# Windowed attention and routed experts on one core: first v queued ahead, gate exp moved behind the third score piece, key copies placed on ScalarE or VectorE by the chunk before, last gate ahead of the row check

## The chip, the core and the metric

The kernel runs on one core of a Trainium2 chip. The time is that of one execution on the device, in microseconds; shorter is better. Engine names are those of the profile: PE is TensorE's matmul, PEld its weight load, DVE is VectorE, ACT is ScalarE, POOL is GpSimd, SP is SyncE.

## The reference

There are 8 batches of 8 heads, 576 positions and head size 64. Attention is causal with a window of 64 positions; its output becomes a row of 512 per position. Then each batch as a whole goes to one of 8 experts, chosen by the mean of its rows. All inputs and the output are float32.

```python
rel = pos[:, None] - pos[None, :]
mask = (rel >= 0) & (rel < 64)
scores = np.where(mask, scale * q @ k.T, -1e9)
attn = exp(scores - max) / (sum + 1e-9)
x = (attn @ v) as (B, S, 512)
...
logits = x.mean(axis=1) @ w_gate
e = argmax(logits); gate_w = softmax(logits)[e]
out[b] = gate_w[b] * (relu(x[b] @ w1[e]) @ w2[e])     # w1 512x1024, w2 1024x512
```

## The kernel before

**Units.** The attention is cut into 16 units u, two for each batch (four heads each, as two pairs s). For a unit, `load_qk` brings q and k as bfloat16 over POOL's DMA queue. `transpose_qk` transposes them on PE into one PSUM tile each, and `leave_qk` copies that tile out: q always on ACT, k on DVE unless ACT is passed. `scores(u, c)` makes the scores of a third (piece) c of the window blocks, and ACT takes the exp of each piece into `pt` (L389). The window is applied in one of two ways: units 0 and 1 add a large negative number on PE before the scores (`add_outside`, into the same PSUM tile); the others multiply the exp by 0 or 1 on DVE (L391, with `masks` from `make_masks`). `values(u, s)` is the second product, of `pt` with v; its 65th column is the row sum, and `norm` divides on DVE (L427, L429) and writes x.

**v.** `load_v(b)` loads a batch's v as float32 over SP's queue. A small POOL instruction first writes one element of the tile, so that the DMA waits for POOL at that place. `cast_part` converts it to float16 twice, in two alignments: "whole" (`va`), and "low" and "high" (`vb`); `cast_v` does all three for a unit.

**Gate.** `transpose_x` transposes x for the expert, ACT summing each row on the way out (`pooled`), and `gate_parts` multiplies the sums with the gate's weights. For batch 0 `pool_mm` and `pool_parts` do this in another way, ahead of the transposes. `gate(b)` finishes the logits with a matmul into PSUM (L488), takes the maximum and its index on DVE (L492 to L495), and loads the index into a POOL register, with which `load_w1` and `load_w2` ask for that expert's weights. `gate_weight(b)` takes the exp and the sum of the logits on ACT (L515) and the reciprocal on DVE (L517). The expert's relu (L562) scales by it.

**Experts.** `expert_chunks` yields, batch after batch, 8 `expert_up` chunks (64 matmuls of 128x288 in all, relu on ACT) and 5 `expert_down` chunks (the output copied by DVE, L575 and L587, and stored over SP's queue). `experts(pace)` issues the next chunks of this stream, so that expert work fills PE between the pieces of attention.

**Order.** Every instruction is kept in program order on its engine (`P`), so the order of the text is the order of each engine's queue. A hand-written lead-in takes units 0 to 3 and the first gate; it holds `busy(n)`, matmuls on zeros that only occupy PE. Then a loop over t handles unit t's scores and values, the transposes of unit t+1, the transpose of x of unit t-1, and at even t (from 6 on) the gate of batch t/2 - 1. At t = 16 (`NU`) there is no unit left; the last gate is done, and `row_check` tests all row sums on DVE for a general fallback, which is not taken here. All PSUM tiles come from one pool of four:

```python
psum = ctx.enter_context(
    tc.tile_pool(name="psum", bufs=4, space=bass.MemoryType.PSUM))
```

so a fifth tile must wait until one of the four is read out.

Of the kernel before, what the change touches and what calls it, by code (L numbers as in the profile page):

```python
# [156 lines left out]
def kernel(  # L157
# [61 lines left out]
    def load_v(b, behind=None):  # L219
        vn = vpool.tile([128, NM, D], FP32, tag="vn")  # L220
        if behind is None:

            P(nc.gpsimd.memset(vn[:, 0, 0:1], 0.0))
        else:

            P(nc.gpsimd.tensor_copy(out=vn[:, 0, 0:1], in_=behind))
        P(nc.sync.dma_start(out=vn, in_=vv[b]))
        v_tiles[b] = vn

    HM = NM // 2  # L230

# [123 lines left out]
    sp_ps = {}  # L355

    def add_outside(u, c):

        sp = psum.tile([128, 2, 512], FP32, tag="ps", name="sp")
# [4 lines left out]
        sp_ps[u, c] = sp  # L364

    def scores(u, c):
        qT, kT = qt_tiles[u], kt_tiles[u]
        masked = (u, c) in sp_ps
        if not masked:
            sp_ps[u, c] = psum.tile([128, 2, 512], FP32, tag="ps", name="sp")  # L370
        sp = sp_ps[u, c]
# [114 lines left out]
    def gate(b, both=True):  # L486
        gl = psum.tile([128, 2, 512], FP32, tag="ps")
        P(nc.tensor.matmul(out=gl[:, 0, 0:E], lhsT=onesf, rhs=gparts[b],  # L488
                           start=True, stop=True))
        glog = gl[:, 0, 0:E]  # L490
# [9 lines left out]
        gate_in[b] = gl, gnm  # L500
        if both:
            gate_weight(b)
# [7 lines left out]
    def gate_weight(b):  # L510
        gl, gnm = gate_in[b]
        glog = gl[:, 0, 0:E]
# [53 lines left out]
    def expert_down(b, mt):  # L566
# [3 lines left out]
        if mt < 4:  # L570
# [4 lines left out]
            P(nc.vector.tensor_copy(out=ob, in_=pso[:, 0, :]))  # L575
# [50 lines left out]
    acc = [0.0]  # L626
# [49 lines left out]
    busy(13)  # L676
    transpose_qk(0, 0)
    add_outside(0, 0)
    transpose_qk(0, 1)
# [15 lines left out]
    cast_v(1)  # L695
# [4 lines left out]
    values(0, 0)  # L700
    values(0, 1)
    transpose_qk(2, 0)
    busy(1)
# [5 lines left out]
    busy(1)  # L709
    pool_mm(1)  # L710
    pool_parts()
    gate(0, False)
# [6 lines left out]
    for c in range(3):  # L719
        scores(2, c)  # L720
        if c == 0:
            gate_weight(0)
# [7 lines left out]
    busy(3)  # L730
# [12 lines left out]
    values(3, 1)  # L743
    experts(1.0)
    transpose_qk(4, 0)
    transpose_qk(4, 1)
    experts(1.0)
    transpose_x(3)

    for t in range(START + 1, NU + LAG):  # L750
# [22 lines left out]
        if t == NU:  # L773
            okc = row_check()
# [3 lines left out]
        if t == START + 1:  # L778
            next_gate()
        if ahead and t > 5:  # L780
            cast_part(t + 1, "low")
        if on:
            scores(t, 1)
        if ahead and t > 5:
            cast_part(t + 1, "high")
        experts(pace)
        if START + 1 < t <= NU and t % 2 == 0:
            next_gate()
        if on:
            scores(t, 2)  # L790
        if t == START + 1:
# [8 lines left out]
        if ahead:  # L800
            transpose_qk(t + 1, 1)
# [47 lines left out]
```

## Time and profile before

| | |
|---|---|
| Time, median of 3 runs | 235.32 us (233.7 to 235.49) |
| Time of the profiled execution | 234.69 us |
| Its span, first to last instruction | 233.0 us |
| Mean granted TensorE clock | 0.981 |
| PE busy | 205.6 us (88%) |
| PE weight load busy | 142.2 us (61%) |
| DVE busy | 140.1 us (60%) |
| ACT busy | 122.5 us (53%) |
| POOL busy | 41.2 us (18%) |
| DMA | 45.64 MB, mean 196 GB/s |

All times in the traces are counted from the start of the span. The time of the execution is 1.69 us longer than its span. A row of the timeline has start, duration, engine, line, operation, output<-inputs, and in brackets how long the engine stood idle before it and what ended that. A row of the groups ends with busy time and mean duration in ns, then the idle time before, and for whom.

### The profile page before, as it was taken

Reading aid. Unit: us, or ns where it says so; the run is one execution under the profiler, and the core shown is the slowest. Engines: PE = TensorE matmul, PEld = TensorE weight load, DVE = VectorE, ACT = ScalarE, POOL = GpSimd, SP = SyncE. Lnnn points to the kernel's source line nnn. Section 1 sums busy time; section 2 is a strip of 40 time slices with the busy share of each in tenths; the row PEclk is TensorE's granted clock in tenths of the full one; section 3 lists DMA queues with packets and bytes.
Section 4 is the critical chain, followed back from the end, with each engine's and each line's share of the span. In section 5 each row is a group of like instructions: output and inputs, shape, how many; then the busy total and the mean of one; then the engine's idle time right before and its main releaser. Section 6 shows DMA issues by size and latency. Waiting matters only on the chain.

```text
span 233.0 us, 6978 instructions
## 1 busy us (share of the span) xinstructions
PE 205.6 (88%) x3012; PEld 142.2 (61%) x3012; DVE 140.1 (60%) x314; ACT 122.5 (53%) x206; POOL 41.2 (18%) x69
## 2 busy tenths in 40 slices
PE   7656889999799899989999899999998999979970
PEld 2335767745587557855686457856686568639630
DVE  2639596578757777478656777467766672440140
ACT  2344686851668338670957356853677247406300
POOL 7146260055000330025000700020002000200000
PEclk9999599999999999999999999999999999999998
DMA  5999899999999999989999799989911993299231
GB/s 62 242 255 234 134 183 219 246 248 224 230 236 262 263 201 245 231 242 173 238 228 299 132 226 234 251 211 220 258 56 11 204 240 114 26 225 245 89 130 67
DMA packets 29910, 45.64 MB, mean 196 GB/s; under 512 B 2480, under 2 KB 21936, under 8 KB 29872
## 3 DMA queue, kind: packets, MB, share of 16 engines
q0 software_dynamic: 13840, 26.22, 62.8%
q1 hardware_dynamic: 15232, 18.88, 26.9%
q8 instruction: 25, 0.41, 0.7%
q10 hardware_dynamic: 800, 0.03, 0.2%
q14 instruction: 13, 0.11, 0.1%
HBM read 61.90 MB, written 9.44 MB: 306 GB/s over the span
## 4 chain that ended last, share of the span: by engine, by line
PE 50%; DMA 17%; ACT 14%; DVE 13%; issue 3%; POOL 1%; POOLq 0%; ACTq 0%
PE php L558 22%; DMA w1t<-in_moe_w_dram 13%; PE pso L572 13%; ACT xT L458 4%; DMA kn<-in_k_dram 4%; ACT pt L389 4%; PE tp L334 4%; PE op L413 4%; ACT hT L562 3%; PE tp L450 3%; DVE x L429 2%; DVE pt L391 2%; PE sp L374 2%; PE pso L581 2%; DVE dst L303 2%
## 5 line engine op out<-in xcount | busy, mean ns | idle before, releaser
L558 PE MATMUL php<-xT,w1t 128*128 128x288 f16 x512 | 71.6, 288 | 3.3 <-DMA w1t<-in_moe_w_dram 2.2
L562 ACT ACTIVATE hT<-php,gatew 128x576 f16<-128x576 f32 x64 | 47.5, 747 | 32.0 <-PE php L558 31.5
L572 PE MATMUL pso<-w2t,hT 128*128 128x512 f16 x256 | 60.2, 380 | 1.9 <-DVE ob L575 0.8
L558 PEld LDWEIGHTS <-w1t 128*128 128x128 f16 x512 | 54.6, 115 | 10.4 <-DMA w1t<-in_moe_w_dram 3.0
L389 ACT ACTIVATE pt<-sp 128x768 f16<-128x768 f32 x48 | 37.7, 814 | 10.0 <-PE sp L374 10.0
L572 PEld LDWEIGHTS <-hT 128*128 128x128 f16 x256 | 23.1, 98 | 27.6 <-issue 2.4
L575 DVE COPY ob<-pso 128x512 f32<-128x512 f32 x32 | 22.0, 688 | 23.5 <-PE pso L572 23.4
L458 ACT ACTIVATE xT<-tp 128x576 f16<-128x576 f16 x28 | 17.9, 647 | 32.6 <-PE tp L450 32.6
L535 POOL DMA_DIRECT2D w1t<-in_moe_w_dram x7 | 5.0, 717 | 143.8 <-DVE gatew L517 102.7
L391 DVE TENSOR_TENSOR pt<-pt,masks 128x768 f16<-128x768 f16 x42 | 23.3, 555 | 9.8 <-ACT pt L389 9.1
L429 DVE TENSOR_TENSOR x<-op,linv 128x640 f16<-128x640 f32 x32 | 26.4, 825 | 1.1
L303 DVE COPY dst<-tp 128x1152 bf16<-128x1152 bf16 x14 | 19.0, 1356 | 8.7 <-PE tp L334 8.6
L347 ACT COPY dst<-tp 128x1152 bf16<-128x1152 bf16 x16 | 17.9, 1122 | 9.0 <-PE tp L334 9.0
L413 PE MATMUL op<-vb,pt 128*64 128x65 f16 x320 | 16.8, 196 | 4.5 <-DVE pt L391 1.4
L413 PEld LDWEIGHTS <-pt 128*64 128x64 f16 x640 | 13.5, 110 | 11.0 <-issue 6.2
L374 PE MATMUL sp<-dst 64*64 64x128 bf16 (+1 forms) x672 | 16.0, 219 | 2.8 <-DVE dst L303 1.1
L374 PEld LDWEIGHTS <-dst 64*64 64x64 bf16 x672 | 10.9, 110 | 9.8 <-issue 5.0
L413 PE MATMUL op<-va,pt 128*64 128x65 f16 x320 | 16.5, 197 | 0.0
L480 DVE SCALAR_TENSOR_TENSOR gpart<-wg,pooled,gpart 128x8 f32<-128x8 f32 x21 | 4.8, 227 | 18.5 <-ACT xT L458 18.4
L303 DVE COPY vb<-va 64x1152 f16<-64x1152 f16 (+1 forms) x30 | 13.9, 464 | 0.6
L450 PE MATMUL tp<-identh,x 128*128 128x128 f16 x160 | 12.6, 231 | 1.5 <-DVE x L429 1.1
L450 PEld LDWEIGHTS <-x 128*128 128x128 f16 x160 | 10.7, 104 | 4.2 <-DVE x L429 2.9
(70 smaller groups left out, 165.5 us busy)
## 6 DMA issues: line engine op xcount, KB each, us to landing
w2t<-in_moe_w_dram POOLq DMA_DIRECT2D x8, 1024.0 KB, 16.4
out_dram<-ob SPq DMA_DIRECT2D x32, 256.0 KB, 8.1
w1t<-in_moe_w_dram POOLq DMA_DIRECT2D x7, 1024.0 KB, 8.9
qn<-in_q_dram POOLq DMA_DIRECT2D x16, 288.0 KB, 12.8
kn<-in_k_dram POOLq DMA_DIRECT2D x16, 288.0 KB, 14.5
w1t<-in_moe_w_dram POOLq DMA_DIRECT2D x2, 512.0 KB, 6.4
out_dram<-ob SPq DMA_DIRECT2D x16, 64.0 KB, 6.9
vn<-in_v_dram SPq DMA_DIRECT2D x8, 0.2 KB, 19.5
```

The source lines that it names most:

```text
L303: P(eng.tensor_copy(out=out, in_=in_))
L374: P(nc.tensor.matmul(out=sp[64 * half:64 * half + 64, s, 64 * (qblk - 6 * c):64 * (qblk - 6 * c) + n], lhsT=kT[64 * s:64 * s + 64, ts(kblk ...
L389: P(nc.scalar.activation(out=pt, in_=sp[:, :, 0:384], func=AF.Exp, scale=scale))
L391: P(nc.vector.tensor_tensor(out=pt, in0=pt, in1=masks[:, c].rearrange("p s g w -> p s (g w)"), op=ALU.mult))
L413: P(nc.tensor.matmul(out=op[64 * half:64 * half + 64, xx, 65 * jj:65 * jj + 65], lhsT=pt[:, s, 64 * (g % 6):64 * (g % 6) + 64], rhs=win, s ...
L429: P(nc.vector.tensor_tensor(out=x[:, :, h0 * D:(h0 + 2) * D].rearrange("p j (x c) -> p x j c", x=2), in0=view[:, :, :, 0:64], in1=li[:, :, ...
L450: P(nc.tensor.transpose(out=tp[:, kl, ts(jj, 128)], in_=x[:, jj, x_chunk(b, kb)], identity=identh))
L458: P(nc.scalar.activation(out=xT[:, kb, :], in_=tp[:, kl, 0:S], func=AF.Copy, accum_out=pooled[:, b, kb:kb + 1]))
L558: P(nc.tensor.matmul(out=php[:, sc, 0:288], lhsT=w1t[:, kb, cols], rhs=xT[:, kb, ts(sc, 288)], start=(kb == 0), stop=(kb == KB - 1)))
L562: P(nc.scalar.activation(out=hT[:, ft].rearrange("p (sc s) -> p sc s", sc=2), in_=php[:, :, 0:288], func=AF.Relu, scale=gatew[:, b:b + 1]))
L572: P(nc.tensor.matmul(out=pso[:, 0, :], lhsT=hT[:, fb, ts(mt, 128)], rhs=w2t[:, fb, :], start=(fb == 0), stop=(fb == FB - 1)))
L575: P(nc.vector.tensor_copy(out=ob, in_=pso[:, 0, :]))
```

## The change

- The first v is asked for ahead of everything else, with no POOL instruction in front; it used to be issued between the first q and the first k.
- In the lead-in: key copies of unit 0 go to ACT; the second v waits for the first k's landing in place of its transposed copy; q and k of units 2 to 4 are asked for together; the casts of the first v are all on DVE, ahead of the second unit's transposes; unit 0's values come before unit 1's scores; the masks are made behind the first gate; the fillers are other in number and size.
- `gate` copies the logits from PSUM to SBUF on DVE and works on the copy; `gate_weight` is always called apart. In the loop it now stands behind the third piece (`scores(t, 2)`); before it followed the index at once.
- The key copy of unit t+1 in the loop goes to `free[0]`: to DVE if the last expert chunk was an `expert_up`, to ACT if it was an `expert_down`. The output copy of `expert_down` 1 goes to ACT.
- At t = 16 the gate comes one `experts(pace)` earlier, and `row_check` behind it.
- At the end of the lead-in `transpose_qk(4, 0)` and `transpose_x(3)` each move ahead of an expert chunk.

```diff
@@ load_qk, load_v @@
         P(nc.gpsimd.dma_start(out=qn, in_=qv[u]))
-        if u == 0:
-            load_v(0)
         P(nc.gpsimd.dma_start(out=kn, in_=kv[u]))
...
-        if behind is None:
+        if b == 0:
+
+            pass
+        elif behind is None:
...
+    load_v(0)
@@ gate @@
-        glog = gl[:, 0, 0:E]
+        glog = small.tile([128, E], FP32, tag="glog")
+        P(nc.vector.tensor_copy(out=glog, in_=gl[:, 0, 0:E]))
...
-        gate_in[b] = gl, gnm
-        if both:
-            gate_weight(b)
+        gate_in[b] = glog, gnm
@@ expert_down @@
-            P(nc.vector.tensor_copy(out=ob, in_=pso[:, 0, :]))
+            copy_on(nc.scalar if mt == 1 else nc.vector, ob, pso[:, 0, :])
@@ expert_chunks, experts @@
-                yield (lambda b=b, ft=ft: expert_up(b, ft)), 1.0
+                yield (lambda b=b, ft=ft: expert_up(b, ft)), 1.0, nc.vector
...
-                yield (lambda b=b, mt=mt: expert_down(b, mt)), (1.7 if mt < 4 else 0.9)
+                yield (lambda b=b, mt=mt: expert_down(b, mt)), (1.7 if mt < 4 else 0.9), nc.scalar
...
+            free[0] = nxt[2]
@@ busy @@
-    def busy(n):
+    def busy(n, cols=128):
...
-            P(nc.tensor.matmul(out=sp[:, 0, :], lhsT=spin[:, 0:128], rhs=spin,
-                               start=True, stop=True))
+            P(nc.tensor.matmul(out=sp[:, 0, 0:cols], lhsT=spin[:, 0:128],
+                               rhs=spin[:, 0:cols], start=True, stop=True))
@@ lead-in @@
-    busy(13)
+    busy(16, 512)
     transpose_qk(0, 0)
     add_outside(0, 0)
-    transpose_qk(0, 1)
+    busy(8)
+    transpose_qk(0, 1, leave=False)
+    leave_qk(0, 1, A)
     add_outside(0, 1)
     add_outside(0, 2)
 
-    load_v(1, kt_tiles[0][:, 0:1])
+    load_v(1, qk_tiles[0][1][:, 0, 0:1])
     load_qk(2)
+    load_qk(3)
+    load_qk(4)
     for c in range(3):
         scores(0, c)
-    make_masks()
+    cast_v(0)
+    cast_v(1)
     transpose_qk(1, 0)
+    busy(6)
     transpose_qk(1, 1)
-    cast_part(0, "high", nc.gpsimd)
-    cast_part(0, "low", nc.gpsimd)
-    load_qk(3)
-    load_qk(4)
-    cast_part(0, "whole")
-    cast_v(1)
+    values(0, 0)
+    values(0, 1)
     for c in range(3):
         add_outside(1, c)
     for c in range(3):
         scores(1, c)
-    values(0, 0)
-    values(0, 1)
     transpose_qk(2, 0)
-    busy(1)
+    busy(12)
     values(1, 0)
     values(1, 1)
     pool_mm(0)
     transpose_qk(2, 1, leave=False)
     leave_qk(2, 1, A)
-    busy(1)
+    busy(8)
     pool_mm(1)
     pool_parts()
-    gate(0, False)
+    busy(5)
+    gate(0)
+    make_masks()
     load_w1(0)
     load_w2(0)
...
     for c in range(3):
         scores(2, c)
-        if c == 0:
-            gate_weight(0)
+    gate_weight(0)
+    busy(4)
...
-    busy(3)
+    busy(12)
...
     values(3, 1)
+    transpose_qk(4, 0)
     experts(1.0)
-    transpose_qk(4, 0)
     transpose_qk(4, 1)
+    transpose_x(3)
     experts(1.0)
-    transpose_x(3)
@@ loop over t @@
-        if t == NU:
-            okc = row_check()
         if on:
             scores(t, 0)
         experts(pace)
         if t == START + 1:
             next_gate()
+        if t == NU:
+            next_gate()
+            gate_weight(B - 1)
+            okc = row_check()
...
         if on:
             scores(t, 1)
+        if t == START + 1:
+            gate_weight(t // 2 - 1)
...
-        if START + 1 < t <= NU and t % 2 == 0:
+        if START + 1 < t < NU and t % 2 == 0:
             next_gate()
         if on:
             scores(t, 2)
+        if START + 1 < t < NU and t % 2 == 0:
+            gate_weight(t // 2 - 1)
...
         if ahead:
-            transpose_qk(t + 1, 1)
+            transpose_qk(t + 1, 1, leave=False)
+            leave_qk(t + 1, 1, free[0])
```

More of the change, by code (lines that the diff above doesn't have):

```diff
@@ L353, in leave_qk, with score_tile @@
             kt_tiles[u] = dst
-    sp_ps = {}
+    sp_ps, on_pe = {}, set()
+    def score_tile(u, c):
+        if (u, c) not in sp_ps:
+            sp_ps[u, c] = psum.tile([128, 2, 512], FP32, tag="ps", name="sp")
+        return sp_ps[u, c]
     def add_outside(u, c):
-        sp = psum.tile([128, 2, 512], FP32, tag="ps", name="sp")
+        sp = score_tile(u, c)
+        on_pe.add((u, c))
         for s in range(2):
@@ L363, in add_outside @@
                 rhs=outside[:, c].rearrange("p g w -> p (g w)"), start=True, stop=False))
-        sp_ps[u, c] = sp
     def scores(u, c):
         qT, kT = qt_tiles[u], kt_tiles[u]
[L368 to L371, printed above, removed]
+        masked = (u, c) in on_pe
+        sp = score_tile(u, c)
         def mm(s, half, kblk, qblk, n):
@@ L484, with gate @@
     gate_in = {}
-    def gate(b, both=True):
-        gl = psum.tile([128, 2, 512], FP32, tag="ps")
+    def gate(b):
+        gl = psum.tile([128, 2, 512], FP32, tag="ps", name="gl")
         P(nc.tensor.matmul(out=gl[:, 0, 0:E], lhsT=onesf, rhs=gparts[b],
                            start=True, stop=True))
-        glog = gl[:, 0, 0:E]
+        glog = small.tile([128, E], FP32, tag="glog")
+        P(nc.vector.tensor_copy(out=glog, in_=gl[:, 0, 0:E]))
         gmx = small.tile([128, 8], FP32, tag="gmx")
@@ L510, in gate_weight @@
     def gate_weight(b):
-        gl, gnm = gate_in[b]
-        glog = gl[:, 0, 0:E]
+        glog, gnm = gate_in[b]
         gex = small.tile([128, E], FP32, tag="gex")
```

2 lines of the change are left out of this document (1 added, 1 removed).

## The prediction

> **What bounds the kernel now.** I read the windows first, for where TensorE (PE) stands idle, then the timeline of those places, then the groups for prices.
>
> ```profile
> span 233.0 us, 6978 instructions
> core 0: us, PE busy (x) PEld busy (x) DVE busy (x) ACT busy (x) POOL busy (x), PEclk, DMA share, GB/s
> 0.00:33.00 33.00, 22.81 (x464) 15.19 (x464) 19.75 (x56) 16.06 (x22) 15.82 (x30) 0.90 0.98 183
> 33.00:62.00 29.00, 26.33 (x421) 18.47 (x410) 21.47 (x46) 17.61 (x32) 8.08 (x13) 1.00 1.12 232
> 88.00:208.00 120.00, 115.33 (x1658) 80.49 (x1657) 77.36 (x170) 67.89 (x120) 12.99 (x20) 1.00 0.87 193
> ```
>
> From 88 to 208 us PE is busy in 115.33 of 120 us, so no reordering can win more than 4.7 us there. The first 33 us hold 10.2 us of idle PE, but what counts in them is the chain to the first expert's weights. It runs like this:
>
> ```profile
> 2.42 51.17 SPq L227 DMA_DIRECT2D vn<-in_v_dram  x5
> 14.49 0.69 PE L334 MATMUL tp<-ident,kn 128*64 128x128 bf16 x18 [1.64 <-DMA kn<-in_k_dram]
> 15.22 1.36 DVE L303 COPY dst<-tp 128x1152 bf16<-128x1152 bf16 x1 [3.78 <-PE tp L334]
> 15.36 2.89 POOL L303 CAST vb<-vn 64x1088 f16<-64x1088 f32 x2 [2.90 <-DMA vn<-in_v_dram]
> 16.50 2.37 DVE L303 CAST va<-vn 128x1152 f16<-128x1152 f32 x2
> 16.64 0.71 PE L374 MATMUL sp<-dst 64*64 64x64 bf16 x42 [0.37 <-DVE dst L303]
> 17.05 2.22 ACT L389 ACTIVATE pt<-sp 128x768 f16<-128x768 f32 x3 [2.92 <-PE sp L374]
> 23.25 0.82 DVE L429 TENSOR_TENSOR x<-op,linv 128x640 f16<-128x640 f32 x1
> 26.12 0.17 DVE L495 TENSOR_SCALAR eidx<-graw 128x8 uint32<-128x8 uint32 x1
> 27.54 1.51 POOL L532 DMA_DIRECT2D w1t<-in_moe_w_dram  x2 [6.37 <-issue]
> 33.06 2.15 PE L558 MATMUL php<-xT,w1t 128*128 128x288 f16 x16
> ```
>
> The second k lands at 14.49 and the first v at 15.36; then VectorE (DVE) works through k copy, casts and four normalizations until 24.08; the expert's index is there at 26.29, its weights are asked for at 27.54, and the first expert matmul follows at 33.06. So every us by which the index comes sooner or later moves what comes after it.
>
> **The change, part by part.** *First v ahead of all.* Its DMA was issued at 2.42 behind POOL's memset; without the memset it can go at about 1.0, 1.4 us sooner (an estimate: the other engines' first instructions start there). What the head start is worth depends on the share that it gets.
>
> ```profile
> 2.00:4.00 2.00, 2.00 (x6) 0.70 (x5) 0.42 (x4) 0.36 (x2) 1.92 (x6) 1.00 0.70 48
> 8.00:12.00 4.00, 2.16 (x64) 1.42 (x64) 2.37 (x7) 1.71 (x3) 1.21 (x3) 1.00 1.16 241
> ```
>
> From 2 to 4 us the DMA engines moved only 48 GB/s, later 241, so there is room in front. The first v (1.18 MB in 12.9 us, 91 GB/s) may gain nothing (lands at 15.36), shift by 1.4 (13.96), or use the room fully: 1.4 us at 241 GB/s is 0.34 MB, at its own 91 GB/s worth 3.7 us (11.7). I take the middle of the two ends, 13.5.
>
> *The order after it.* All six casts of the first v now go to DVE, ahead of the second k's copy, and PE does the first unit's second products before it opens the second unit's score tiles. With four PSUM tiles (the pool's bufs=4), k's tile and two product tiles are held, so the third score tile must wait for the first normalization, and the scores stand behind it in PE's order. Chain from the landing of v, from these rows:
>
> ```profile
> L303 DVE CAST va<-vn x16: 750/754/1702, 16.5 to 173.7; 128x1152 f16<-128x1152 f32 x16
> L303 DVE COPY vb<-va 64x1152 f16<-64x1152 f16 (+1 forms) x30 | 13.9, 464 | 0.6
> L427 DVE RECIPROCAL linv<-op 128x10 f32<-128x10 f32 x32 | 6.9, 215 | 6.8 <-PE op L413 6.8
> ```
>
> Casts 2 x 0.754 + 4 x 0.464 = 3.36; k copy 1.36; first normalization 0.215 + 0.82 = 1.04; mask matmuls and the first third of the scores 0.6 (an estimate: a third of the 0.71 at 16.64, the same for the masks, and the handovers); three exps 2.22; the last products 0.3; two normalizations 2.08: 11.0 us to the last one. From there to the index it took 26.29 - 24.08 = 2.21, and the new copy of the logits adds 0.17 (as the 128x8 operation at 26.12). The index comes 13.4 us after v. At 13.5 that is 26.9: **0.6 us later**, break-even at 12.9. Bounds: with v at 15.36, 28.8, so +2.5; if v is early the second k rules (14.49 + 0.69 + 11.0 - 3.36 + 2.4), 25.2, so -1.1.
>
> The casts are priced at 0.754, not at the 1.19 that the pair at 16.50 took while POOL cast beside it; with 1.19 the chain would be 0.86 longer. [...]
>
> The fillers (three more matmuls ahead of the first transposes, more later) delay q and k copies by under 1 us, hidden by the wait for v and the second k. The masks, now made on DVE behind the gate (six small operations, at the 0.17 of 26.12 about 1 us), must be there before the third unit's first multiplication; it is paid by the w1 transfer (27.54 to 33.06), within which DVE also did its work before. If that cover is gone they cost that 1 us.
>
> *From 33 to 62.*
>
> ```profile
> 49.27 0.71 POOL L535 DMA_DIRECT2D w1t<-in_moe_w_dram  x1 [14.30 <-DVE gatew L517]
> 61.62 1.17 PE L558 MATMUL php<-xT,w1t 128*128 128x288 f16 x8 [0.86 <-DMA w1t<-in_moe_w_dram]
> ```
>
> The second expert's w1 is late by 0.86. The last transpose_x of the lead-in moves ahead of one expert chunk, so this gate can come some 1 us earlier; the DMA share is 1.12 here, so part of it stays in the queue. I take -0.4 (bounds -0.86 and 0).
>
> *The gate's exp behind the third piece, logits in SBUF.*
>
> ```profile
> ACT gex L515 <- DVE gnm L498: 8.9, 7, 2.4
> 104.28 0.22 PE L413 MATMUL op<-vb,pt 128*64 128x65 f16 x1 [0.78 <-DVE pt L391]
> 129.71 0.22 PE L413 MATMUL op<-vb,pt 128*64 128x65 f16 x1 [0.65 <-DVE pt L391]
> 153.47 1.89 PE L572 MATMUL pso<-w2t,hT 128*128 128x512 f16 x8 [0.46 <-ACT gex L515]
> 177.79 1.14 PE L558 MATMUL php<-xT,w1t 128*128 128x288 f16 x8 [0.45 <-ACT gex L515]
> 102.57 0.27 ACT L515 ACTIVATE gex<-gl,gnm 128x8 f32<-128x8 f32 x1 [1.23 <-DVE gnm L498]
> ```
>
> ScalarE (ACT) stands 1.3 us on average before each gate's exp, and behind it stands the third piece's exp, whose multiplication PE waits for (0.78, 0.65); or PE waits for the PSUM tile that the exp holds (0.46, 0.45). After the change the third exp starts some 1.3 us sooner, and DVE's copy frees the tile before the index is even searched. The third multiplication then waits only for DVE's gate chain, 0.17 longer, and is done a little before PE comes. All four waits go: **-2.34** (bounds -2.34 and, if another wait steps in, 0). The expert weight is computed later, but is first used by the next expert's chunks, whose weights are still to be loaded then.
>
> *Keys on ACT beside second products.*
>
> ```profile
> 134.92 0.73 PE L450 MATMUL tp<-identh,x 128*128 128x128 f16 x10 [0.30 <-DVE x L429]
> 184.30 0.40 PE L450 MATMUL tp<-identh,x 128*128 128x128 f16 x4 [0.30 <-DVE x L429]
> 135.69 0.65 ACT L458 ACTIVATE xT<-tp 128x576 f16<-128x576 f16 x1 [5.62 <-PE tp L450]
> L301 ACT COPY dst<-tp 128x1152 bf16<-128x1152 bf16 x2 | 2.2, 1122 | 2.6 <-PE tp L334 2.6
> ```
>
> Twice PE waits 0.30 for a normalization that stands behind a 1.36 us k copy on DVE. On ACT the copy takes 1.12 and falls into its idle 5.62 us: **-0.6** (bounds -1.0 and 0; without the cover five such copies would put up to 5.6 us before exps). One of five output copies goes the same way; nothing.
>
> *Last gate ahead of the row check.*
>
> ```profile
> 197.97 0.39 PE L488 MATMUL gl<-gpart,onesf 128*128 128x8 f32 x2
> 198.72 0.49 DVE L605 TENSOR_REDUCE okc<-okt 128x1 f32<-128x320 f16 x1
> 199.59 0.17 DVE L495 TENSOR_SCALAR eidx<-graw 128x8 uint32<-128x8 uint32 x1
> 200.84 0.72 POOL L535 DMA_DIRECT2D w1t<-in_moe_w_dram  x1 [21.06 <-DVE gatew L517]
> 206.67 1.90 PE L572 MATMUL pso<-w2t,hT 128*128 128x512 f16 x8
> 209.77 8.03 PE L558 MATMUL php<-xT,w1t 128*128 128x288 f16 x64 [1.20 <-DMA w1t<-in_moe_w_dram]
> ```
>
> The row check ends at 199.21 (198.72 + 0.49), the gate's matmul at 198.36; with a handover of 0.1 on both sides the search starts some 0.7 sooner, less the 0.17 copy 0.5, and the weights land at 209.27. But the gate's matmul also moves ahead of one expert chunk, to about 197.0 (a chunk is an eighth of the 8.03 at 209.77), while its input is ready only at 197.9, just before it ran, so PE loses 0.9 there and ends its old work at 209.5 instead of 208.57. The later of the two decides: **-0.2** (bounds -0.5 and +0.3).
>
> **Sum.** +0.6 - 0.4 - 2.34 - 0.6 - 0.2 = -2.9. The profiled execution took 234.69 us, 0.6 below the median of 235.32 and within the runs shown (233.7 to 235.49), so I leave it as the base: **231.8 us**.
>
> **The rivals.** *v early*: the first v lands at 12 or before, the second k sets the start, -1.1 in place of +0.6: 230.1. For it speaks the empty DMA at 2 to 4 us, against it the shared engines after that. [...]
>
> *v not sooner*: the head start is lost in the slow first us, v still at 15.36, +2.5: 233.7.
>
> *Slower, the start loses more than the rest wins*: the three further q and k pairs are now queued as soon as the first k has landed, two of them formerly behind POOL's casts after 15.36, and the second v stands behind the first. If they cost the first v 2 us, it lands at 17.4, the index 4.5 us later than before: 235.7. It decides from v at 16.4, where the other terms (-3.5) are used up. For it speaks that casts, scores and products all stand behind v now; against it, that POOL's queue was never empty before 14.5 anyway.
>
> *The middle gives nothing*: PE reaches the next w1 before it lands.
>
> ```profile
> 113.44 1.10 PE php L558 x8
> ```
>
> This row of the chain of waits is the fourth expert's first chunk. Its w1 was asked for about 1.2 after the index (as 26.29 to 27.54), at some 103.6, and takes some 8.9 (200.84 to 209.77), so it lands at 112.5, about 0.9 us ahead; a PE that is 0.8 faster is just in time. If it takes all, -2.34 falls away: 234.1.
>
> **How the numbers follow.** Forecast 0.40 (own range 230.8 to 232.8), v early 0.18, v not sooner 0.13, middle gives nothing 0.13, slower 0.16. About 1% (2.35 us) is what a measurement of this kernel can tell from no change, so faster means below 232.97. Faster: 0.35 of the forecast, 0.17 of v early, 0.01 of the rest, 0.53. Slower means above 237.67, which only the slower rival's far end reaches, with v 4 us late: 0.10. Same: 0.37. The range goes from 229.6 (v early with 0.5 more in the middle) to 235.2 (part of the slower rival): some 0.8.
>
> **What would show it.** Right: no idle on ACT before gex, none of the four waits at the gates, first v at 13 to 14, the index at 26.3 to 27.5, the last w1 asked for some 0.5 us earlier relative to its gate matmul. Wrong: index at 25.2 or after 28; new idle of PE before an expert's first matmul; exps on ACT waiting behind key copies; score matmuls of the second unit not waiting for the first normalization.

## The result: no change that can be measured, and the profile after

The changed kernel takes 234.53 us (median of 20 runs, 233.22 to 236.07), the kernel before on the same chip 234.73 us (20 runs, 233.48 to 237.45). The ratio is 1.0002 with an interval of 0.9984 to 1.0019. The gain of 2.9 us that was forecast isn't there. Ratios here leave out disturbed runs and medians don't, so that the two can differ a little.

The profiled execution of after took 236.07 us, the longest of its 20 and 1.5 above the median; its span is 234.3 us, against 233.0 before (234.69 us, at the median). Where that 1.5 is from is told below.

**The start.** The timeline of after, up to the first expert matmul (start, duration, engine, line, operation, and in brackets the idle time ahead and what ended it):

```profile
8.81 0.69 PE L336 MATMUL tp<-ident,qn 128*64 128x128 bf16 x18 [2.13 <-DMA qn<-in_q_dram]
10.94 0.69 PE L336 MATMUL tp<-ident,kn 128*64 128x128 bf16 x18 [0.56 <-DMA kn<-in_k_dram]
11.48 0.76 DVE L305 CAST va<-vn 128x1152 f16<-128x1152 f32 x1 [4.03 <-DMA vn<-in_v_dram]
14.43 1.11 DVE L305 COPY vb<-va 64x1152 f16<-64x1152 f16 x2
17.97 0.50 PE L369 MATMUL sp<-outside,ident 128*128 128x384 bf16 x2 [0.50 <-DVE x L434]
18.40 0.53 PE L379 MATMUL sp<-dst 64*64 64x64 bf16 x27
21.34 0.37 PE L379 MATMUL sp<-dst 64*64 64x64 bf16 x15 [2.41 <-issue]
22.55 1.46 PE L651 MATMUL idle<-spin 128*128 128x128 bf16 x12
25.99 0.82 DVE L434 TENSOR_TENSOR x<-op,linv 128x640 f16<-128x640 f32 x1
27.64 0.23 PE L666 MATMUL pool<-once,x 128*128 128x1 f16 x3 [0.57 <-issue]
29.50 0.17 DVE L502 TENSOR_SCALAR eidx<-graw 128x8 uint32<-128x8 uint32 x1
30.89 1.51 POOL L536 DMA_DIRECT2D w1t<-in_moe_w_dram  x2 [14.90 <-DVE masks L293]
36.31 0.93 PE L562 MATMUL php<-xT,w1t 128*128 128x288 f16 x6 [0.28 <-DMA w1t<-in_moe_w_dram]
```

The first v lands at 11.46 (11.48 here, the cast that waited for it), 3.9 us sooner than before and sooner than I forecast. Yet the index is finished at 29.67, 3.4 us later than the 26.29 of before. In between, PE stands still for 2.41 us in the middle of 42 score matmuls of one kind, with nothing that the profile shows to wait for ("issue"): 27 are done, 15 are not. It happens again, for 0.57, at 27.64.

**The rest.** PE's timeline of after: the first matmul of the second and of the third expert, and the last gate's matmul.

```profile
65.11 1.17 PE L562 MATMUL php<-xT,w1t 128*128 128x288 f16 x8 [1.77 <-DMA w1t<-in_moe_w_dram]
92.60 0.68 PE L562 MATMUL php<-xT,w1t 128*128 128x288 f16 x4 [1.92 <-DMA w1t<-in_moe_w_dram]
200.44 0.39 PE L493 MATMUL gl<-gpart,onesf 128*128 128x8 f32 x2 [0.82 <-DVE gpart L485]
```

Windows of after; behind the engines' busy times stand granted clock, DMA share and GB/s:

```profile
33.00:62.00 29.00, 26.23 (x442) 18.60 (x437) 20.87 (x45) 18.91 (x30) 9.32 (x16) 1.00 1.13 228
88.00:208.00 120.00, 115.55 (x1673) 80.61 (x1671) 70.66 (x168) 78.19 (x134) 12.99 (x20) 0.99 0.90 196
94.00:95.00 1.00, 1.00 (x18) 0.61 (x11) 0.00 (x0) 1.00 (x2) 0.00 (x0) 0.50 1.21 259
96.00:97.00 1.00, 1.00 (x16) 0.72 (x16) 0.00 (x0) 0.61 (x1) 0.00 (x0) 0.51 1.04 223
```

And two rows of before's timeline that the prediction didn't show, the third expert's first matmul and the request for its first weights:

```profile
79.24 0.72 POOL L535 DMA_DIRECT2D w1t<-in_moe_w_dram  x1 [23.76 <-DVE gatew L517]
87.68 1.17 PE L558 MATMUL php<-xT,w1t 128*128 128x288 f16 x8 [0.17 <-DMA w1t<-in_moe_w_dram]
```

From these rows, those of the prediction and the spans the account of the two profiled executions follows, stretch by stretch:

| stretch, by PE | before | after | difference |
|---|---|---|---|
| start to first expert | 33.06 | 36.31 | +3.25 |
| first to second expert | 28.56 | 28.80 | +0.24 |
| second to third expert | 26.06 | 27.49 | +1.43 |
| third expert to last gate's matmul | 110.29 | 107.84 | -2.45 |
| from there to the end of the span | 35.03 | 33.86 | -1.17 |

The sum is +1.3, the difference of the spans. So the middle and the end won 3.6 us, and the start with the two experts behind it gave back 4.9. In the third stretch PE waits 1.92 for the third expert's w1, where it waited 0.17. Behind that wait the granted clock is 0.50 for some 3.4 us (93.6 to 97.0), which costs the fourth stretch about 1.4: without such a dip it took 106.43 us, as will be seen. In the window from 88 to 208 the work that moved is seen: DVE 70.7 us (77.4 before), ACT 78.2 (67.9). The 1.4 is about the 1.5 by which this execution is above the median; that the shorter ones lack the dip is not shown, since only this one was profiled.

### The profile page after: what moved, and what is told of

Read it like the earlier page. It is cut to its first block, busy times and chain, and to the rows that moved or that the text cites. A ratio compares the mean times of both kernels' runs of the same rounds, so it can differ in the third digit from the quotient of the medians.

```text
span 234.3 us, 7103 instructions
## 1 busy us (share of the span) xinstructions
PE 209.0 (89%) x3065; PEld 146.0 (62%) x3065; DVE 128.3 (55%) x309; ACT 135.4 (58%) x221; POOL 38.1 (16%) x66
## 4 chain that ended last, share of the span: by engine, by line
PE 62%; DMA 16%; ACT 11%; DVE 5%; issue 3%; POOLq 0%; SPq 0%
PE php L562 24%; PE pso L576 19%; DMA w1t<-in_moe_w_dram 12%; PE tp L336 6%; PE op L418 5%; DMA vn<-in_v_dram 4%; ACT xT L463 4%; ACT pt L394 3%; ACT hT L566 3%; PE pso L585 2%; PE tp L455 2%; PE sp L379 2%; DVE vb L305 1%; PE idle L651 1%; DVE va L305 1%
## 5 line engine op out<-in xcount | busy, mean ns | idle before, releaser
L562 PE MATMUL php<-xT,w1t 128*128 128x288 f16 x512 | 72.5, 291 | 4.6 <-DMA w1t<-in_moe_w_dram 4.0
L305 DVE COPY ob<-pso 128x512 f32<-128x512 f32 x24 | 16.5, 689 | 25.9 <-PE pso L576 25.8
L349 ACT COPY dst<-tp 128x1152 bf16<-128x1152 bf16 x16 | 17.9, 1116 | 9.2 <-PE tp L336 9.1
L379 PE MATMUL sp<-dst 64*64 64x128 bf16 (+1 forms) x672 | 16.1, 221 | 3.9 <-issue 2.4
L432 DVE RECIPROCAL linv<-op 128x10 f32<-128x10 f32 x32 | 7.0, 217 | 21.3 <-PE op L418 21.3
L418 PE MATMUL op<-vb,pt 128*64 128x65 f16 x320 | 16.5, 199 | 1.5 <-DVE vb L305 1.4
L305 DVE COPY vb<-va 64x1152 f16<-64x1152 f16 (+1 forms) x32 | 15.2, 475 | 0.5
L303 ACT COPY dst<-tp 128x1152 bf16<-128x1152 bf16 x9 | 10.1, 1119 | 9.0 <-PE tp L336 8.8
L305 DVE CAST va<-vn 128x1152 f16<-128x1152 f32 x16 | 12.6, 787 | 4.5 <-DMA vn<-in_v_dram 4.4
## 6 DMA issues: line engine op xcount, KB each, us to landing
w2t<-in_moe_w_dram POOLq DMA_DIRECT2D x8, 1024.0 KB, 16.9
kn<-in_k_dram POOLq DMA_DIRECT2D x16, 288.0 KB, 15.5
```

Of the source, the lines that this page charges most:

```text
L305: P(eng.tensor_copy(out=out, in_=in_))
L349: P(nc.scalar.copy(out=dst.rearrange("p (x r t) -> p x r t", x=2, t=NT), in_=view))
L379: P(nc.tensor.matmul(out=sp[64 * half:64 * half + 64, s, 64 * (qblk - 6 * c):64 * (qblk - 6 * c) + n], lhsT=kT[64 * s:64 * s + 64, ts(kblk ...
L418: P(nc.tensor.matmul(out=op[64 * half:64 * half + 64, xx, 65 * jj:65 * jj + 65], lhsT=pt[:, s, 64 * (g % 6):64 * (g % 6) + 64], rhs=win, s ...
L562: P(nc.tensor.matmul(out=php[:, sc, 0:288], lhsT=w1t[:, kb, cols], rhs=xT[:, kb, ts(sc, 288)], start=(kb == 0), stop=(kb == KB - 1)))
```

## The experiments

Each is compared with the kernel before on the same chip. The first two cut the change in two, the next five are about the pause, the last three about single parts.

**The change without its lead-in, and its lead-in alone.** In e1 the place of the first v and the whole lead-in up to the first experts are the old ones; gate, keys and last gate are the new ones. In e2 it is the other way round.

```diff
@@ e1: after, with the lead-in of before @@
-    load_v(0)
...
+        if u == 0:
+            load_v(0)
...
-    busy(16, 512)
+    busy(13, 512)
...
-    cast_v(0)
-    cast_v(1)
+    make_masks()
     transpose_qk(1, 0)
-    busy(6)
     transpose_qk(1, 1)
-    values(0, 0)
-    values(0, 1)
+    cast_part(0, "high", nc.gpsimd)
+    cast_part(0, "low", nc.gpsimd)
...
@@ e2: before, with the lead-in of after @@
+    load_v(0)
...
```

> The changed kernel with the old lead-in and the old place of the first v; gate, key copies, last gate and the order at the end of the lead-in stay changed. Theory (the lead-in eats what the rest wins): the four waits at the gates stay gone, php of the first expert at 33.1 as before, time 2 to 2.7 us under before, about 232.2. Rival (the rest wins nothing, PE only runs into the next w1): within 0.5 us of before, with 1.5 us or more of new waiting for w1 at the second to fourth expert.

> The kernel before with the new lead-in and the first v ahead of all, nothing else. Theory: the first expert starts some 3 us later than before (36 in place of 33.1) although the first v lands 4 us sooner; time 2 to 3 us over before, about 237. Rival (the lead-in is neutral, the late start of the profiled execution was an exception): first expert at 33 to 34, time within 0.7 of before.

e1: 231.86 us, ratio 0.9858 (0.9803 to 0.9913): **1.4% faster than before.** That is the lowest ratio of all variants, but not told apart from those of e3, e5 and e11 below. e2: 237.23 us, ratio 1.0107 (1.0057 to 1.0157). So the rest of the change wins, and the lead-in loses; the two ratios multiply to 0.9963, and with their intervals that is not told apart from the 1.0002 of both together. In e1's timeline the first expert begins at about its old time (its profiled execution, 233.78 us, is the longest of its six):

```profile
33.35 2.15 PE L560 MATMUL php<-xT,w1t 128*128 128x288 f16 x16 [0.74 <-DMA w1t<-in_moe_w_dram]
```

In e2's the pause returns, at the same matmul:

```profile
21.25 0.36 PE L376 MATMUL sp<-dst 64*64 64x64 bf16 x15 [0.81 <-issue]
27.28 0.23 PE L662 MATMUL pool<-once,x 128*128 128x1 f16 x3 [1.46 <-issue]
```

e2 has the old gate and still pauses with 15 scores and then with 3 pool matmuls to go, like after. So the pause belongs to a place in PE's program.

**What is at that place?** Counted in PE's rows of the trace, the 2.41 comes behind 223 matmuls and the 0.57 behind 351. A matmul stands in the trace as two rows, a weight load and a product (3,065 of each in after), so the two places are 256 rows apart. In the other four variants that pause (e2 to e5) 223 matmuls are done too. The page of after has among its DMA queues one for instructions (packets, MB, share of 16 engines):

```profile
q8 instruction: 26, 0.43, 0.7%
```

26 packets of together 0.43 MB are some 16.5 KB each (16,384 bytes in the trace). PE's rows in the trace, 6,130 in all, are 24 blocks of 256: about as many. The DMA view of a narrow window finds the single packet, here from 18.6 to 18.7 us of after:

```profile
q8 instruction: 1, 0.02, 77.8%
```

There a block begins to arrive, and PE goes on at 21.34, 2.7 us later. The next one begins at 25.3, and PE goes on at 27.64, 2.3 later. In before the packet came at 14.3, and PE passed the same row of its program at about 19.0 without a pause. The theory: PE's program comes in blocks of 256 instructions over the same DMA engines as the data (the view counts q8's packets in the time of the same 16); with the data queues full (DMA share 1.11 from 16 to 20 us of after) a block is late, and the new lead-in, which runs through its instructions faster and has more of them (fillers, earlier products), reaches the end of the block before the next is there. The 256 is the distance of the two pauses; that a packet of q8 is a block of PE's program is inferred from its time and from the two counts, since no view says whose instructions a packet holds.

**Fewer fillers, so that other instructions stand at the boundary.** e3 leaves out 14 filler matmuls ahead of the place, e5 leaves out 17 (and 12 more behind it, ahead of the second unit's products).

```diff
@@ e3: after, without @@
-    busy(8)
-    busy(6)
@@ e5: as e3, and @@
-    busy(16, 512)
+    busy(13, 512)
-    busy(12)
```

> The changed kernel without the fillers busy(8) and busy(6) in the first 15 us (14 matmuls, 28 instructions less). Theory (PE stands because its next block of 256 instructions is not there yet): PE stands again, but 14 matmuls further on in its program, 15 scores of the second unit then being done, that is in the q transposes of unit 2; the second unit's exps are no longer held up by it, the index comes 1 to 2 us sooner than 29.7, time 0.5 to 1.5 under the changed kernel. Rival (the scores wait for something of their own, a tile or a copy): the gap stays after the 27th matmul of the second unit's scores and the time does not change by more than 0.3.

> The changed kernel without busy(8), busy(6) and busy(12), and with busy(13) at the start: 17 matmuls fewer ahead of the second unit's scores, 29 ahead of its values. Theory (PE's program comes in blocks of 256 instructions): PE stands after the second of the q transposes of unit 2, no longer within the second unit's scores; their three exps run in one piece; index 1.5 to 2.5 us sooner than the 29.7 of the changed kernel, time 1.5 to 3 under it, about 232. Rival (fillers keep the clock up and are needed): granted clock 0.5 over more of 21 to 33 us than in the changed kernel, time no lower than that of the run without busy(8) and busy(6), 232.4.

e3: 232.37 us, ratio 0.9877 (0.9824 to 0.993). e5: 232.18 us, ratio 0.988 (0.9845 to 0.9914). PE's timeline of e3:

```profile
21.82 0.19 PE L379 MATMUL sp<-dst 64*64 64x64 bf16 x1 [1.63 <-issue]
```

And that of e5:

```profile
19.63 0.25 PE L336 MATMUL tp<-ident,qn 128*64 128x128 bf16 x2 [0.36 <-DMA qn<-in_q_dram]
21.72 0.64 PE L336 MATMUL tp<-ident,qn 128*64 128x128 bf16 x16 [1.84 <-issue]
```

The pause moves by exactly the number of matmuls left out: in e3 it stands ahead of the last score, 41 instead of 27 done; in e5 three further, behind two of the q transposes. (For e3 I had written "in the q transposes"; 15 scores were left and 14 were taken out, so it fell one short.) No data, tile or semaphore moves like that: it is the place in the program. The packets begin at 19.4 in both, and PE goes on some 2.4 later. Both are 1.2% faster than after, more than the start shows: the index comes at 29.18 in e3 (0.5 sooner than in after, less than the 1 to 2 expected) and at 28.01 in e5 (1.7 sooner, as expected), and the first expert begins at 35.77 and 35.42, 0.5 and 0.9 sooner. The rival's sign for e5 came true as well, a low clock over more of the start:

```profile
23.50:33.00 9.50, 9.20 (x141) 8.27 (x142) 6.56 (x25) 5.35 (x10) 3.76 (x5) 0.50 0.67 107
```

That is PE's clock at 0.50 from 23.5 to 33 us of e5, so with fewer fillers the clock was lower there (in after it is 0.61 from 21 to 25 us, 0.93 from 25 to 29 and 0.61 from 29 to 33), and by time e5 is not told apart from e3. In e3's profiled execution the rest is at the third expert, whose w1 is waited for 0.94 instead of 1.92, with no fall of the clock behind it.

**Less data in the queues.** e4 asks for q and k of units 3 and 4 only behind the second unit's key copy (about 17 us), e7 asks for these and the second v behind the first normalization (about 18 us). One thing more follows from e7's edit: the second v's wait no longer stands in POOL's queue ahead of q and k of unit 2, which so go out at 5.97 instead of 11.48, and this q lands at 15.51 instead of 20.30.

```diff
@@ e4: after, with @@
-    load_qk(3)
-    load_qk(4)
...
     transpose_qk(1, 1)
+    hold = const.tile([128, 1], BF16)
+    P(nc.gpsimd.tensor_copy(out=hold, in_=kt_tiles[1][:, 0:1]))
+    load_qk(3)
+    load_qk(4)
@@ e7: after, with @@
-    load_v(1, qk_tiles[0][1][:, 0, 0:1])
     load_qk(2)
-    load_qk(3)
-    load_qk(4)
...
     values(0, 1)
+    load_v(1, x_tiles[0][:, 0, 64:65])
+    load_qk(3)
+    load_qk(4)
```

> The changed kernel with q and k of units 3 and 4 asked for only behind the second unit's key copy (17 us in place of 13 to 16). Theory A (the block of instructions comes late because more transfers are queued beside it): the gap of 2.4 us in the second unit's scores shrinks to under 1.2, index 1.5 to 2 sooner, time 1 to 1.5 us under the changed kernel. Theory B (it comes late because PE gets through a block faster than any fetch under a full DMA, whatever is queued): gap within 0.5 us of 2.4, time within 0.4 of the changed kernel.

> The changed kernel with the second v and q, k of units 3 and 4 asked for only behind the first normalization (18 us), so that from some 15 to 18 us the DMA engines have little to do while PE's next block is due. Theory A (the block is late because the DMA engines are full): the gap after the 27th matmul of the second unit's scores shrinks from 2.4 to under 0.6 us, index 2 us sooner. Theory B (a block takes its 6 to 8 us anyway): gap 1.5 or more.

e4: 234.2 us, ratio 0.9968 (0.9935 to 1.0001); the pause is 1.89, and its packet begins at 18.0. Theory A's sign (under 1.2) failed, and this is nearly what theory B expected. So the two pairs alone are not what fills the queues; by e4 alone the question would stay open. e7: 232.74 us, ratio 0.9925 (0.9896 to 0.9953). The windows of after and then of e7 from 16 to 20 us:

```profile
16.00:20.00 4.00, 2.25 (x56) 1.14 (x49) 2.83 (x5) 1.30 (x2) 0.00 (x0) 1.00 1.11 240
```

```profile
16.00:20.00 4.00, 3.31 (x98) 2.20 (x92) 2.89 (x5) 1.68 (x3) 1.60 (x4) 1.00 0.07 14
```

The DMA view of e7 from 16.1 to 16.2 us, and from its timeline the 42 scores in one piece, the index and the first expert:

```profile
q8 instruction: 1, 0.02, 60.9%
```

```profile
18.46 0.71 PE L379 MATMUL sp<-dst 64*64 64x64 bf16 x42
25.53 0.17 DVE L502 TENSOR_SCALAR eidx<-graw 128x8 uint32<-128x8 uint32 x1
34.03 1.39 PE L562 MATMUL php<-xT,w1t 128*128 128x288 f16 x5 [2.45 <-DMA w1t<-in_moe_w_dram]
```

With the queues nearly empty (share 0.07 instead of 1.11; the last queued pair lands at 15.5 and 16.9) the block begins to arrive 2.5 us sooner, at 16.1, and both pauses are gone. The index is there at 25.70, 4.0 us sooner than in after and 0.6 sooner than in before. **This shows the cause: the same program, in the same order on PE, doesn't pause when the data stay out of the way.**

Both halves of the theory can be read from PE's rows and the packets. In after PE passes the place 256 rows ahead of the pause at 13.2 us, and the packet begins 5.4 us later; in e7 it is 13.3 and 2.8, in before 11.0 and 3.3. For the 256 rows themselves PE takes 5.5 us in e7 (13.3 to 18.8), but 8.0 in before (11.0 to 19.0). PE went on no sooner than 2.3 us after its packet began wherever it paused, so a lag of 5.4 is too much for a PE that takes 5.5, and before's 3.3 is not for one that takes 8.0. That a block is asked for at just this place, 256 rows ahead, is inferred: with the queues empty the packet follows it by 0.5 us (e8) and 0.7 (e7's second block).

But the transfers only went elsewhere: the first w1, asked for at 26.93, is behind them and lands at 34.0, and PE waits 2.45 for it.

**Can the late transfers be kept out of w1's way as well?** e9 is e7 with q and k of unit 4 asked for behind the first expert's weights.

```diff
@@ e9: e7, with @@
     load_qk(3)
-    load_qk(4)
...
     load_w1(0)
     load_w2(0)
+    load_qk(4)
```

> As the run with the light DMA, but q and k of unit 4 are asked for only behind the first expert's weights, so that these no longer queue behind them. Theory (the block of instructions no longer comes late, and the first w1 finds a nearly empty queue): no gap in the second unit's scores, index near 25.5, first expert at 31.5 to 33 in place of 34.0, time 1 to 2 us under that run and at or under the run with the old lead-in, 231 to 232. Rival (the DMA engines are the bound up to the third expert, whatever the order): the wait for w1 moves to the second or third expert and the time stays at 232.7 within 0.5.

235.09 us, ratio 1.0013 (0.9983 to 1.0043). The first expert comes at 33.43, within what was expected, but the time meets neither forecast: the q of unit 4, now asked for at 30.32, is missed:

```profile
45.38 0.69 PE L336 MATMUL tp<-ident,qn 128*64 128x128 bf16 x18 [2.32 <-DMA qn<-in_q_dram]
```

In e7 and e9 what was put off was missed later, by 2.45 us for the first w1 and by 2.32 for the q of unit 4: by these two runs the transfers bound this lead-in.

**v first in the old order.** e8 is e1 with the first v ahead of all and its casts on DVE ahead of the second unit, nothing else of the new lead-in.

```diff
@@ e8: e1, with @@
+    load_v(0)
...
     make_masks()
+    cast_v(0)
+    cast_v(1)
     transpose_qk(1, 0)
     transpose_qk(1, 1)
-    cast_part(0, "high", nc.gpsimd)
-    cast_part(0, "low", nc.gpsimd)
     load_qk(3)
     load_qk(4)
-    cast_part(0, "whole")
-    cast_v(1)
```

> The old lead-in with two parts of the new one: the first v ahead of all, and its casts all on DVE ahead of the second unit's key copy; PE's order and fillers as in the old lead-in; all else as in the changed kernel. Theory (v first is worth its head start where PE does not first run into a block boundary or a tile held by the first products): first v lands at 11 to 13, index at 24.3 to 25.5 in place of 26.3, time 1 to 2 us under the run with the old lead-in (231.9), about 230.5. Rival (the second k or PE's blocks set the start): index at 26 or later, time within 0.7 of 231.9.

233.81 us, ratio 0.996 (0.993 to 0.999), 1.0% behind e1. Neither forecast fits: the index comes at 28.53, later than in e1 (26.74), and the time is 1.9 over e1's. There is no pause, and v is early (11.24), but PE gets the first k at 10.59 instead of e1's 9.42 (8.34 in before), and on DVE the casts now stand ahead of the second k's copy, for which PE waits (the timeline of DVE and PE):

```profile
14.09 0.95 DVE L305 CAST va<-vn 128x1152 f16<-128x1152 f32 x1
18.40 1.36 DVE L305 COPY dst<-tp 128x1152 bf16<-128x1152 bf16 x1
19.82 0.76 PE L379 MATMUL sp<-dst 64*64 64x64 bf16 x42 [2.03 <-DVE dst L305]
```

Here an early v with its casts ahead of the second unit brings nothing by itself, and while v comes sooner the first k comes 1.17 us later than in e1.

**The gate and the keys by themselves.** e10 is e1 with the old gate (logits in PSUM, exp at once in the loop, also at the last gate); e11 is e1 with every key copy and the second output copy on DVE, as before.

```diff
@@ e10: e1, with @@
-        glog = small.tile([128, E], FP32, tag="glog")
-        P(nc.vector.tensor_copy(out=glog, in_=gl[:, 0, 0:E]))
+        glog = gl[:, 0, 0:E]
...
+            gate_weight(b)
...
             scores(t, 2)
-        if START + 1 < t < NU and t % 2 == 0:
-            gate_weight(t // 2 - 1)
@@ e11: e1, with @@
-            copy_on(nc.scalar if mt == 1 else nc.vector, ob, pso[:, 0, :])
+            P(nc.vector.tensor_copy(out=ob, in_=pso[:, 0, :]))
-            leave_qk(t + 1, 1, free[0])
+            transpose_qk(t + 1, 1)
```

> The run with the old lead-in (231.9), with the gate as in the kernel before: logits left in PSUM, exp straight behind the index. Theory (the four waits at the gates are worth 2.3 us): they are back at 0.78, 0.65, 0.46 and 0.45, time 1.8 to 2.8 us over the run with the old lead-in. Rival (the gain comes from elsewhere): within 0.7 of it.

> The run with the old lead-in (231.9), with all key copies of the loop and the output copies of expert_down 1 back on DVE. Theory: two waits of 0.30 for a normalization are back, time 0.3 to 1.0 us over the run with the old lead-in. Rival (ACT's own queue is the worse place): time under it.

e10: 233.16 us, ratio 0.995 (0.9918 to 0.9982). Against e1, through the kernel before on each chip, that is 0.6% by the medians and 0.9% by the ratios, so the gate is worth 1.3 to 2.2 us. The four waits are back in PE's timeline, and the waits for w1 at the third and fourth expert, which e1 has, are nearly gone. e10:

```profile
87.83 1.17 PE L559 MATMUL php<-xT,w1t 128*128 128x288 f16 x8 [0.18 <-DMA w1t<-in_moe_w_dram]
104.43 0.22 PE L416 MATMUL op<-vb,pt 128*64 128x65 f16 x1 [0.79 <-DVE pt L394]
129.86 0.22 PE L416 MATMUL op<-vb,pt 128*64 128x65 f16 x1 [0.64 <-DVE pt L394]
153.15 1.89 PE L573 MATMUL pso<-w2t,hT 128*128 128x512 f16 x8 [0.45 <-ACT gex L516]
177.48 1.14 PE L559 MATMUL php<-xT,w1t 128*128 128x288 f16 x8 [0.45 <-ACT gex L516]
197.18 0.39 PE L491 MATMUL gl<-gpart,onesf 128*128 128x8 f32 x2 [0.82 <-DVE gpart L483]
```

And e1 at these two experts:

```profile
90.01 1.17 PE L560 MATMUL php<-xT,w1t 128*128 128x288 f16 x8 [0.80 <-DMA w1t<-in_moe_w_dram]
116.18 0.88 PEld L560 LDWEIGHTS <-w1t 128*128 128x128 f16 x8 [1.54 <-DMA w1t<-in_moe_w_dram]
```

e11: 231.83 us, ratio 0.9884 (0.9847 to 0.9922), not told apart from e1. Two waits of 0.29 and 0.30 for a normalization are back, as expected, but 0.6 us is less than these times resolve: by time the keys' worth isn't shown.

The stretch from the third expert to the last gate's matmul tells more. It was 110.29 in before and 107.84 in after; in e7 and e3 the clock doesn't fall there. e7:

```profile
89.19 1.17 PE L562 MATMUL php<-xT,w1t 128*128 128x288 f16 x8 [1.73 <-DMA w1t<-in_moe_w_dram]
195.62 0.39 PE L493 MATMUL gl<-gpart,onesf 128*128 128x8 f32 x2 [0.82 <-DVE gpart L485]
```

And e3:

```profile
90.90 1.17 PE L562 MATMUL php<-xT,w1t 128*128 128x288 f16 x8 [0.94 <-DMA w1t<-in_moe_w_dram]
197.34 0.39 PE L493 MATMUL gl<-gpart,onesf 128*128 128x8 f32 x2 [0.82 <-DVE gpart L485]
```

That is 106.43 and 106.44. In e10 it is 109.35 (its first and sixth row above). So in this stretch the new gate wins 2.9 us, and the keys with the last gate's place another 0.94 (110.29 to 109.35). Against e1 itself, which has e10's lead-in, the gate wins only 1.44 there: e1's stretch is 107.91, since PE stands 1.40 for the fourth expert's w1 (its weight load 1.54, in the row above). So in e1 half of the gate's gain goes into the next transfer. In e11, which waits 1.31 at that place, the stretch is 108.78: by this one pair of executions the keys are worth 0.9.

## Why the prediction was wrong

**The start** (+0.6 forecast, bounds -1.1 and +2.5; +3.25 measured). The landing of v wasn't the error: 11.46 lies below even the 11.7 I gave for full use of the idle queue. By "the index 13.4 after v" it would have come at 24.9; by the second bound, the second k, at 25.2. It came at 29.67, 18.2 after v. The step that failed is this chain from v to the index, above all by a term that it lacked, the wait for PE's own program. Four terms were missing or too small:

- The wait for a block of PE's program: 2.41 and 0.57. I had no term for it at all, because before shows no such pause. e7 shows about what it weighs: without the two pauses, and the low clock behind them, the index is there at 25.70, 14.0 after its v (11.66), close to the 13.4 forecast. That is 4.2 us less than in after; up to 1.2 of it can be the earlier q of unit 2, for which PE, without the pause, would have stood from 19.1 (as in e7) to 20.3 (an estimate from these rows).
- The six casts: 4.06 us (11.48 to 15.54) for 3.36. The second big cast took 0.99, not 0.754, and the low and high copies 0.55, not 0.464. The first big one took 0.76. POOL, which casts nothing here, was issuing the DMAs of q and k from 11.48 to 15.98. In the twelve traces all 147 casts of this size with no POOL instruction beside them take 0.75 to 0.76; all that take more than 0.77, up to 1.70, have a POOL cast or DMA issue beside them (though not each cast with one is slow), and in e8 one takes 0.95 at a DMA share of 0.03. So the slower casts go with POOL's work, its DMA issues too, and not with the load of the DMA engines. That with POOL's casts gone both big casts cost 0.754 was my estimate, which no run had shown; beside POOL's DMA issues they took 0.76 and 0.99. The 0.7 decided little: in e7, where POOL issues nothing beside them, the six take 3.5, and the k copy behind them begins at 15.63, no sooner than the 15.57 of after, since PE's transposes of the second k end only then.
- The fillers, which I took as hidden: behind the pause the clock is 0.50, and twelve of them take 1.46 us (0.83 in e7) ahead of the second unit's products, which the chain waits for.
- The head start itself. The first q begins on PE at 8.81 instead of 6.76, the first k at 10.94 instead of 8.34. That v's head start leaves q and k where they were was my assumption (the bound takes the second k at its old 14.49), and my sum has no term for them; here they came 2.0 and 2.6 us later. In e8 an early v, with its casts ahead of the second unit, costs more than it brings.

The third score tile waiting for the first normalization was right (PE stands 0.50 for it).

**33 to 62** (-0.4 forecast, +0.24 measured). The second expert's w1 is not less late but more, 1.77 instead of 0.86; e1 too has 1.96. Counted from the first expert's first matmul, the request came only 0.14 sooner (52.38 - 36.31 = 16.07, before 49.27 - 33.06 = 16.21), not the 1 us that I gave it, and the transfer took 12.7 instead of 12.3, at a DMA share of 1.13 in the window. I had taken the middle between -0.86 and 0; the other side of zero wasn't among the bounds.

**62 to 92** (no term; +1.43). The third expert's w1 is asked for at 83.16. Counted from the second expert's first matmul that is 18.05 us; before it was 79.24 - 61.62 = 17.62. The copy of the logits, 0.17, which I charged to the first and last gate, sits here too, and another 0.25 lies between index and request (1.36 instead of 1.12). The transfer took 9.4 instead of 8.4 us. PE had no slack there: it waited 0.17 already, a row that I didn't quote. My rival "the middle gives nothing" had this mechanism, but I tested it on the fourth expert, where 0.9 was spare. The 0.25 comes with the gate's change: this time between index and request is 1.10 and 1.11 in e2 and e10, with the old gate, and 1.31 to 1.37 in after and the eight other runs with the new one. In the traces of after and e1 the request follows the reciprocal of the expert weight; that this is what holds it up is not shown.

**The gate** (-2.34) **and the keys** (-0.6): right. All four waits and both of the keys' waits are gone from after. The stretch won 2.9 and 0.94 where the clock doesn't fall in it, a little more than the waits add up to; what the 0.6 beyond the gate's four waits is made of stays open. One sign of the prediction was missed without harm: ACT still stands 5.2 us in all before these exps (8.9 before), but PE no longer waits for what is behind them. After itself shows 2.45 in all, since the clock dip behind the third expert's wait took 1.4.

**The last gate** (-0.2): right. PE waits 0.82 at the gate's matmul, I had said 0.9, and the last w1 is waited for no longer. The stretch behind it is shorter by 1.17, but some 0.8 of that lies behind the last output copy, which begins 7.2 us ahead of the end of the span in before and 6.4 in after; I had no term for it. Before, then after:

```profile
225.84 0.69 DVE L575 COPY ob<-pso 128x512 f32<-128x512 f32 x1 [1.40 <-PE pso L572]
```

```profile
227.90 0.69 DVE L305 COPY ob<-pso 128x512 f32<-128x512 f32 x1 [1.40 <-PE pso L576]
```

The account for an execution without the dip is an estimate from these rows: +3.25 + 0.24 + 1.43 - 2.45 - 1.4 - 1.17 = -0.1 us; the medians differ by -0.2.

**The rivals.** "v early" had the right event and the wrong end: v at 11.5, and still no gain. "The start loses more than the rest wins" named what happened, but its mechanism, a late v from 16.4 on, was not the one. "The middle gives nothing" has the nearest time, 234.1, by luck: it takes away the gate's 2.34, and that was won. It is also luck that the time lies within the range that I gave, since losses at the start that I didn't foresee and gains that I did cancel.

## What to carry to other kernels

When a change makes a tensor engine run through its instructions faster or adds small ones, count them. In after, with the data queues full (DMA share 1.11), the packet taken for the next 256 rows began only 5.4 us after PE had passed the place 256 rows ahead, and PE stood for 2.41; in the trace this is an idle "issue" in the middle of a run of equal matmuls. In this lead-in the transfer that went first was paid for by the others (v 3.9 us sooner, q and k 2.0 and 2.6 later), so follow the chain of all of them and not only of the one that moved. And where a row already shows a wait of 0.2 for a transfer, there is no slack: every tenth put ahead of its request counts (the third expert's w1, waited for 0.17 in before and 1.92 in after), and a faster engine only waits longer (in e1 1.40 of the gate's gain).

## What was new about the hardware

- Queue q8 moved 26 packets of 16,384 bytes in after, for 24 blocks of 256 of PE's rows; I take them for PE's program. PE went on 2.3 to 2.7 us after such a packet began, in all five kernels that paused. The packet began 0.5 to 0.7 us after PE passed the place 256 rows ahead of the boundary where the queues were empty (e8, e7), and 5.4 us after it in after, where they were full (DMA share 1.11).
- A wait of PE of 1.92 us at 92.60 was followed by 3.4 us at a granted clock of 0.50, and one of 2.41 at 21.34 likewise; one of 1.77 at 65.11 was not. With e7's 2.45 at 34.03 the clock fell to 0.50 too, and behind e4's 1.81 at 91.43, but not behind e9's 1.82 at 92.01. In before it was 0.50 from 24 to 29 us, behind no pause of this kind but a wait of 1.22 at 21.18. So the length of the wait alone doesn't tell whether the clock falls; what does is not shown.
- With 1.5 us of head start (issued at 0.93 instead of 2.42) the first v landed 3.9 us sooner, and the first q and k 2.0 and 2.6 us later. In the twelve traces the first v landed at 15.2 to 16.7 us in the old place and at 11.2 to 12.5 in the new, the first k at 8.3 to 9.4 and at 10.6 to 11.8.
- DVE's cast of 128x1152 took 0.75 to 0.76 us in all 147 cases of the twelve traces with no POOL instruction beside it (12 of 16 in before and 12 of 16 in after); each longer one, up to 1.70, had a POOL cast or DMA issue beside it.
